# A fused transformer block: the first stage in another order, and Q scaled in whole half-groups

## The chip, the cores and the metric

The kernel runs on one core of one Trainium2 chip. The core has a matrix engine (TensorE, PE in the profile), a vector engine (VectorE, DVE), an activation engine (ScalarE, ACT), GpSimd (POOL), a queue engine (SyncE, SP) and 16 DMA engines. Each engine runs its own list of instructions in order and waits at semaphores for the others. The metric is device time in microseconds for one launch: the median of 3 runs of the kernel before is 843.28 us (843.05 to 843.71).

## The reference

Inputs are in bfloat16: tokens x of 2048 by 1024, a conditioning vector c, and the weights. The block is

```python
mod = (_silu(c) @ w_mod).reshape(c.shape[0], 6, 1, -1)
sa, ca, ga, sb, cb, gb = ...                     # six vectors of 1024
h = _layernorm(x) * (1 + ca) + sa
x = x + ga * _A_ref(h, A_wqkv, A_wo)             # linear attention, 32 heads of 32
h = _layernorm(x) * (1 + cb) + sb
x = x + gb * _B_ref(h, B_w_gate, B_w_up, B_w_down)   # gelu(h@w_gate) * (h@w_up) @ w_down, F = 3584
```

The attention has no softmax. With phi(t) = (t + 1 if t > 0 else exp(t)) + 1e-6, each head forms kv = phi(K)^T V (32 by 32) and z = the sum of phi(K) over tokens, and its output is phi(Q) kv / (phi(Q) z + 1e-6), which goes through wo.

## The kernel before

The 2048 tokens lie in SBUF as 16 chunks of 128 (`XALL`); four chunks make a token group of 512 (`sg` 0 to 3). The kernel keeps a list of instructions for each engine. A small scheduler (`Sched`) records which bytes each instruction reads and writes and derives the semaphore waits; the order on each engine is the order in which the Python code emits the instructions. Nothing reorders them later. DMAs go through SP; each takes one of 8 lanes in turn and waits for the DMA before it on its lane. DMAs issued from ACT would take one of 2 lanes.

**First stage (lines 429 to 746).** SP issues c, the first four token chunks one by one, `w_mod` in quarters (`wmq_dma(q)`: 256 columns of the shift and 256 of the scale, two DMAs of 512 KB), the K weights `wk` in row pairs, the V weights `wv` in column halves. For each of chunks 0 to 3, DVE computes layer norm statistics (`ln1_bn`, twice for a chunk, and `ln1_fin`), POOL raises the variance to -0.5, DVE normalises (`xhat_dve`), PE transposes (`t1`, eight 128 by 128 transposes into one PSUM bank), ACT copies the result into `H1` (L521), and DVE applies the modulation to it row tile by row tile (`mod1`, L538). The modulation vectors come quarter by quarter from PE (`mod_cols(q)`, 32 one-column matmuls, bank 4) and DVE (`mod_copy`). With quarter q, row tiles 2q and 2q+1 of the K projection can run: `k_part(q, chunks)`. Seven of the eight 128 by 512 K tiles of chunks 0 to 3 accumulate in banks 0 to 3 and 5 to 7 over all quarters; the eighth (chunk 3, second half) uses bank 4. `warm(n)` issues n matmuls of zeros on PE. When a K tile is whole, `k_evac` computes phi: ACT exp (L601), DVE min (L602), DVE add (L604). Then the V tiles follow in banks 0 to 3 in turn (`kv_mm`, `v_evac`), and `kvacc` accumulates kv and z in banks 5 to 7.

**Middle.** Chunks 4 to 15 repeat K, V and kvacc, with two 128 by 512 Q blocks for each chunk (`q_block`, evacuated by phi into `PQ[sg]`).

**Scaling of Q (lines 848 to 917).** Twelve Q blocks remain. `den` computes phi(Q) z for two token groups on PE, DVE inverts it (L854), SP stores the reciprocals to DRAM and loads them again broadcast over partitions into `RB[sg % 2]` (`rb_load`, L867, eight DMAs of 256 KB for a group, four for each half of its tokens). `pq_scale(sg, h, gs)` multiplies half h of group sg by them: one DVE instruction (L880) for two of the eight head groups, so four for a whole half. `kvbd` masks kv to its block diagonal (three DVE instructions), `kvt` transposes it (eight PE transposes in bank 4 and an ACT copy), and `w2_pair(g)` folds it into wo (two PE matmuls, an ACT copy into `W2`).

**Output projection (lines 932 to 988).** `wo_chunk(c)` runs 16 matmuls for each chunk, in banks 6 and 7 for chunk 0 and then in banks 2 and 3 or 0 and 1 in turn; DVE adds the result to `XALL` (L941), which frees the banks. For chunks 0 to 3, ACT and POOL compute the second layer norm and SP issues a DMA transpose into `H2` (`ln2_a`, T2). After chunk 9 DVE applies the second modulation (`mod2`). Chunks 12 to 15 are projected later, between gate/up pairs.

**Feed-forward.** For each group 28 tiles of gate and up (`ffn_fc`, L1003 and L1006) and the down projection (`ffn_down`, L1031), with the weights streamed by SP.

Of the kernel before, what the change touches and what calls it, by code (L numbers as in the profile page):

```python
# [12 lines left out]
D = 1024  # L13
# [201 lines left out]
def bass_adaLN_cond__linear_attn_block__geglu_ffn__prompt_kernel(  # L215
# [15 lines left out]
    with ExitStack() as es:  # L231
# [79 lines left out]
        def r_sm(name):  # L311
            return [(SMO[name], SMO[name] + SMSZ[name], name)]
# [7 lines left out]
        def r_xs(c0, c1):  # L320
            return [(OFF_XALL + c0 * D * 2, OFF_XALL + c1 * D * 2, "xall")]
# [104 lines left out]
            gop(lambda e, k=k: e.memset(bm32f[32 * k:32 * (k + 1), 8 * k:8 * k + 33 * 7 + 1:33], 1.0), wr=r_sm("bm32"))  # L426


        sch.dma(Q, lambda e: e.dma_start(C8[:], c_v), wr=r_sm("c8"), note="c8")

        def x_dma(c0, c1):
            return sch.dma(Q, lambda e: e.dma_start(XALL[:, c0:c1, :], x_v[:, c0:c1, :]), wr=r_xs(c0, c1), note=f"x{c0}")
# [14 lines left out]
        sch.op(V, lambda e: e.memset(ADD4[:, 0:2], 0.0), wr=r_sm("add4"), note="add4")  # L447
        sch.op(V, lambda e: e.memset(ADD4[:, 2:4], 1.0), wr=r_sm("add4"), note="add4")
        x_dma(0, 1)
        x_dma(1, 2)  # L450
        wmq_dma(0, (1,))
        x_dma(2, 3)
        wmq_dma(0, (0,))
        x_dma(3, 4)
        w_dma(WK, OFF_WK, "wk", 1, 0, D, 0, 2)
        for q in range(1, 4):
            wmq_dma(q)
            w_dma(WK, OFF_WK, "wk", 1, 0, D, 2 * q, 2 * q + 2)
        w_dma(WV, OFF_WV, "wv", 2, 0, 512)
        w_dma(WV, OFF_WV, "wv", 2, 512, 1024)  # L460
        x_dma(4, 8)
        w_dma(WQ, OFF_WQ, "wq", 0, 0, 512)
# [203 lines left out]
        def warm(n, bank=None):  # L666
            for _ in range(n):
                sch.op(T, lambda e: e.matmul(PS(0 if bank is None else bank), WARM[:, 0:P], WARM[:, :], start=bank is not None,  # L668
                                             stop=bank is not None, skip_group_check=True),
                       rd=R_WARM, pwr=pr(bank) if bank is not None else (), note="warm")  # L670
# [11 lines left out]

        kb0 = {(0, 0): 0, (0, 1): 1, (1, 0): 2, (1, 1): 3, (2, 0): 5, (2, 1): 6, (3, 0): 7}

        def k_part(q, cs):
            for dc in (2 * q, 2 * q + 1):
                for (c_, jg), b in kb0.items():
                    if c_ in cs:
                        kv_mm(c_, "k", jg, b, [dc])
# [42 lines left out]
        k_part(2, [0, 1, 2])  # L732
        mod_cols(3, 4)
        mod1(0, 4, 6, 8)
        k_part(2, [3])
        warm(2)
        k_part(3, [0, 1, 2, 3])
        for (c_, jg), b in kb0.items():
            k_evac(c_, jg, b)
        kv_mm(3, "k", 1, 4, list(range(NDC)))  # L740
        k_evac(3, 1, 4)
        for c_ in range(4):
            for jg in range(2):
                b = nb()
                kv_mm(c_, "v", jg, b, list(range(NDC)))
                v_evac(c_, jg, b)
            if c_ == 0:
                ln1(4)
                for k, t in enumerate((4, 5, 10, 11)):
                    wm_dma(t, k)  # L750
            if c_ >= 1:
                kvacc(c_ - 1)
            if c_ == 1:
                ln1(5)
            if c_ == 2:
                ln1(6)
                x_dma(12, 16)
                t1d(6)
                t1(4, 4)
                mod1(4, 1)  # L760
# [72 lines left out]
        def w2_pair(g, b0=2):  # L833
            for half in range(2):
                b = b0 + half
                sch.op(T, lambda e, b=b, half=half: e.matmul(PS(b), KVT[:, g, :], WO[:, g, half * 512:(half + 1) * 512], start=True, stop=True),  # L836
                       rd=R_KVT + [(OFF_WS + g * 2048 + half * 1024, OFF_WS + g * 2048 + (half + 1) * 1024, "wo")], pwr=pr(b), note=f"w2 {g}.{half}")
            sch.op(A, lambda e: e.activation(W2[:, g, :], ps_all[:, b0 * 512:(b0 + 2) * 512], ACTF.Copy),
                   prd=pr(b0) + pr(b0 + 1), wr=r_w(OFF_WK, "w2", g), note=f"w2cp{g}")
# [30 lines left out]
                        wr=r_rb(i, h) if k == 0 else (), deps=made[0].deps if k else [o_rd[sg // 2]], note=f"rb{sg}.{h}.{k}"))  # L870
                rb_ops[sg, h] = made

        GH = [((0, 2), (2, 4)), ((4, 6), (6, 8))]

        def pq_scale(sg, h, gs):
            i, t0 = sg % 2, h * HW
            for g0, g1 in gs:
                ap = PQ[sg][:, g0:g1, t0:t0 + HW]
                rng = r_pq(sg, g0, g1, t0, t0 + HW)
                sch.op(V, lambda e, ap=ap, i=i, h=h, g0=g0, g1=g1: e.tensor_tensor(ap, ap, RB[i][:, h, g0:g1, :], ALU.mult),  # L880
                       rd=rng + r_rb(i, h, g0, g1), wr=rng, deps=rb_ops[sg, h], note=f"pqs{sg}.{h}.{g0}")
# [19 lines left out]
        kvbd()  # L901
        q_next()
        q_next()
        for u in range(NG):
            q_next()
            if u == 0:
                kvt()
            else:
                w2_pair(u - 1)
            if u in (2, 3):  # L910
                pq_scale(0, 0, GH[u - 2])
            if u in (5, 6):
                pq_scale(0, 1, GH[u - 5])
        w2_pair(NG - 1, 4)
        assert not q_todo

        wd_q = [0]
# [56 lines left out]
        for c_ in range(12):  # L974
            wo_chunk(c_, 6 if c_ == 0 else 2 * (c_ % 2))
            if c_ == 0:
                den(1, 4)
                rb_load(2)
            if 1 <= c_ <= 8:
                pq_scale(1 + (c_ - 1) // 4, (c_ - 1) // 2 % 2, GH[(c_ - 1) % 2])  # L980
            if c_ == 4:
                rb_load(3)
            if c_ in (10, 11):
                pq_scale(3, 0, GH[c_ - 10])
            if c_ < 4:
                ln2_a(c_, False)
            if c_ == 9:
                mod2(0, 2)
                mod2(2, 2)
# [160 lines left out]
```

## Time and profile before

| what | value |
|---|---|
| median of 3 runs | 843.28 us (843.05 to 843.71) |
| the profiled execution | 843.05 us, its span 841.3 us |
| PE busy | 830.7 us, 99% of the span |
| DVE, ACT, POOL busy | 492.0, 294.9, 24.4 us |
| first V matmul, first output projection, first gate matmul on PE | 31.40, 201.47, 244.00 us |
| fillers (`warm`) on PE | 32, the first twelve from 2.31 us |
| one 128x512 phi: exp, min, add | 0.60, 0.43, 0.69 us |
| one scaling (L880), one addition (L941) | 0.68, 1.22 us |

The span goes from the first to the last instruction of the profiled execution; its own time is 1.75 us longer. All times in the lines below count from the start of the span. A line of the order of time gives start, duration, engine, source line, operation, what is written and read, and how many instructions were merged; in square brackets stand the idle time before it and what ended it. The matmuls overlap on PE, so the pace (start to start) of a 512-column matmul is 0.216 us, although one takes 0.379 us from start to end. "SPq" lines are DMA issues; their duration is that of the issue. A line of the transfers gives the size and the time from issue to landing.

### The profile page before, as it was taken

What the parts mean: (1) busy time and instruction counts of PE and PEld (TensorE: products, weight loads), DVE (VectorE), ACT (ScalarE), POOL (GpSimd) and SP (SyncE); (2) the same over time, 40 slices, a digit from 0 to 9 for tenths busy, and PEclk for the clock granted to TensorE, in tenths of its full rate; (3) what the DMA queues carried; (4) which work ended last, traced back from release to release, by engine and by line L of the source; (5) the groups of instructions that cost most, each with busy time, mean ns of one, the idle gap of its engine ahead of it and who ended that gap; (6) DMA issues with size and microseconds to landing.
All of it is one profiled execution on the core that took longest, in us unless ns stands there. A gap on an engine that the chain in (4) does not pass through costs nothing.

```text
span 841.3 us, 11255 instructions
## 1 busy us (share of the span) xinstructions
PE 830.7 (99%) x4149; PEld 387.9 (46%) x4229; DVE 492.0 (58%) x883; ACT 294.9 (35%) x483; POOL 24.4 (3%) x64
## 2 busy tenths in 40 slices
PE   8999999999999999999999999999999999999998
PEld 4454444444444444444444444444444444444445
DVE  5666767867785555654455665346666535655522
ACT  2343333335513344420355442044444104445300
POOL 2000000000200000010000001000000000000000
PEclk9999999999999999999999999999999999999999
DMA  9991824029778587340555533055553305555000
GB/s 286 354 285 26 263 47 105 14 54 233 165 165 252 155 253 206 105 97 23 149 153 154 153 102 69 26 157 150 150 151 101 75 19 158 152 157 141 7 19 26
DMA packets 181750, 112.70 MB, mean 134 GB/s; under 512 B 33080, under 2 KB 172728, under 8 KB 180672
## 3 DMA queue, kind: packets, MB, share of 16 engines
q1 hardware_dynamic: 181696, 111.98, 49.0%
q8 instruction: 34, 0.56, 0.3%
q14 instruction: 20, 0.16, 0.1%
HBM read 100.67 MB, written 4.47 MB: 125 GB/s over the span
## 4 chain that ended last, share of the span: by engine, by line
PE 96%; DVE 2%; issue 1%; ACT 1%; DMA 0%; ACTq 0%
PE ps_all L1006 23%; PE ps_all L1031 23%; PE ps_all L1003 22%; PE ps_all L612 12%; PE ps_all L934 7%; PE ps_all L653 6%; PE ps_all L668 1%; PE ps_all L634 1%; DVE h1T L538 1%; PE ps_all L584 0%; PE ps_all L836 0%; PE ps_all L565 0%; PE ps_all L519 0%; DVE ww L1019 0%; DVE ww L1016 0%
## 5 line engine op out<-in xcount | busy, mean ns | idle before, releaser
L1006 PE MATMUL ps_all<-h2T,wu 128*128 128x512 bf16 x896 | 339.6, 379 | 2.0
L1003 PE MATMUL ps_all<-h2T,wg 128*128 128x512 bf16 x859 | 325.6, 379 | 0.0
L1031 PE MATMUL ps_all<-wd,yT 128*128 128x512 bf16 (+1 forms) x907 | 193.2, 372 | 0.9
L1014 ACT ACTIVATE q<-ps_all 128x512 f32<-128x512 f32 x112 | 66.9, 597 | 229.4 <-PE ps_all L1003 224.5
L1031 PEld LDWEIGHTS ps_all<-wd,yT 128*128 128x128 bf16 x924 | 90.4, 98 | 103.2
L1003 PEld LDWEIGHTS ps_all<-h2T,wg 128*128 128x128 bf16 x896 | 87.7, 98 | 105.8 <-issue 0.2
L1006 PEld LDWEIGHTS ps_all<-h2T,wu 128*128 128x128 bf16 x896 | 87.7, 98 | 105.6
L1016 DVE SCALAR_TENSOR_TENSOR ww<-q,ps_all 128x512 f32<-128x512 f32 x112 | 77.0, 688 | 88.2 <-ACT guh L1015 88.2
L1019 DVE SCALAR_TENSOR_TENSOR ww<-th,guh 128x512 f32<-128x512 f32 x112 | 77.6, 693 | 77.9 <-ACT th L1018 77.9
L1018 ACT ACTIVATE th<-ww 128x512 f32<-128x512 f32 x112 | 70.5, 630 | 85.8 <-DVE ww L1016 85.8
L1021 DVE TENSOR_TENSOR yT<-ww,ps_all 128x512 bf16<-128x512 f32 x112 | 76.9, 687 | 3.8
L1036 DVE TENSOR_TENSOR ps_all<-ps_all,gbb 128x512 f32<-128x512 f32 (+1 forms) x33 | 22.5, 683 | 94.8 <-PE ps_all L1031 94.8
L1015 ACT ACTIVATE guh<-ps_all 128x512 f32<-128x512 f32 x112 | 66.3, 592 | 0.0
L601 ACT ACTIVATE eb<-ps_all 128x512 f32<-128x512 f32 x64 | 37.5, 601 | 77.9 <-PE ps_all L612 37.8
L653 PE MATMUL ps_all<-h1T,wq 128*128 128x512 bf16 x245 | 56.8, 379 | 1.4 <-DVE pq L604 0.7
L612 PE MATMUL ps_all<-wv,h1T 128*128 128x512 bf16 x254 | 57.8, 379 | 0.2
L612 PE MATMUL ps_all<-wk,h1T 128*128 128x512 bf16 x251 | 57.6, 379 | 0.2
L934 PE MATMUL ps_all<-w,pq 128*128 128x512 bf16 x251 | 56.0, 379 | 0.3
L602 DVE TENSOR_SCALAR eb<-eb 128x512 f32<-128x512 f32 x64 | 27.1, 424 | 34.0 <-ACT eb L601 33.6
L934 PEld LDWEIGHTS ps_all<-w,pq 128*128 128x128 bf16 x256 | 25.0, 98 | 30.2 <-issue 0.2
L612 PEld LDWEIGHTS ps_all<-wv,h1T 128*128 128x128 bf16 x256 | 24.9, 98 | 30.0 <-DVE eb L602 0.6
L612 PEld LDWEIGHTS ps_all<-wk,h1T 128*128 128x128 bf16 x256 | 24.6, 98 | 29.8 <-DVE h1T L538 1.5
(81 smaller groups left out, 398.8 us busy)
## 6 DMA issues: line engine op xcount, KB each, us to landing
wg<-in_B_w_gate_dram SPq DMA_DIRECT2D x56, 512.0 KB, 4.1
wu<-in_B_w_up_dram SPq DMA_DIRECT2D x56, 512.0 KB, 5.3
wmst<-in_w_mod_dram SPq DMA_DIRECT2D x8, 1024.0 KB, 11.6
rb<-scr_rd SPq DMA_DIRECT2D x32, 256.0 KB, 6.9
wd<-in_B_w_down_dram SPq DMA_DIRECT2D x7, 1024.0 KB, 7.6
wmq<-in_w_mod_dram SPq DMA_DIRECT2D x8, 512.0 KB, 7.0
out_dram<-xall SPq DMA_DIRECT2D x31, 128.0 KB, 1.7
xall<-in_A_x_dram SPq DMA_DIRECT2D x3, 1024.0 KB, 11.9
```

Of the source, the lines that this page charges most:

```text
L612: o = sch.op(T, lambda e, dc=dc: e.matmul(PS(bank), H1[sg][:, dc, ci * P:(ci + 1) * P], W_[:, dc, jg * 512:(jg + 1) * 512], start=(dc == 0 ...
L653: o = sch.op(T, lambda e, dc=dc: e.matmul(PS(b), WQ[:, dc, qc * P:(qc + 1) * P], H1[sg][:, dc, :], start=(dc == 0), stop=(dc == NDC - 1)), ...
L934: last[half] = sch.op(T, lambda e, g=g, half=half: e.matmul(PS(b0 + half), PQ[sg][:, g, ci * P:(ci + 1) * P], W2[:, g, half * 512:(half + ...
L1003: og = sch.op(T, lambda e, dc=dc: e.matmul(PS(bg), WG[slot][:, dc, e_ * P:(e_ + 1) * P], H2[sg][:, dc, :], start=(dc == 0), stop=(dc == ND ...
L1006: ou = sch.op(T, lambda e, dc=dc: e.matmul(PS(bu), WU[slot][:, dc, e_ * P:(e_ + 1) * P], H2[sg][:, dc, :], start=(dc == 0), stop=(dc == ND ...
L1014: sch.op(A, lambda e: e.activation(Q1[j][:, :], PS(bg), ACTF.Square, scale=math.sqrt(GELU_A)), prd=pr(bg), wr=rq, note=f"q1 {fc}")
L1015: ogh = sch.op(A, lambda e: e.activation(GUH[j][:, :], PS(bg), ACTF.Copy, scale=0.5), prd=pr(bg), wr=rg, note=f"gh {fc}")
L1016: sch.op(V, lambda e: e.scalar_tensor_tensor(WW[j][:, :], Q1[j][:, :], 1.0, PS(bg), op0=ALU.add, op1=ALU.mult), rd=rq, prd=pr(bg), wr=rw, ...
L1018: sch.op(A, lambda e: e.activation(TH[j][:, :], WW[j][:, :], ACTF.Tanh, scale=GELU_C), rd=rw, wr=rt, note=f"th {fc}")
L1019: sch.op(V, lambda e: e.scalar_tensor_tensor(WW[j][:, :], TH[j][:, :], 1.0, GUH[j][:, :], op0=ALU.add, op1=ALU.mult), rd=rt + rg, wr=rw, n ...
L1021: sch.op(V, lambda e: e.tensor_tensor(YT[:, fc, :], WW[j][:, :], PS(bu), ALU.mult), rd=rw, prd=pr(bu), wr=r_yt(fc), note=f"yT {fc}")
L1031: o = sch.op(T, lambda e, b=b, fc=fc, c0=c0, c1=c1, n=n: e.matmul(PS(b, 0, n), YT[:, fc, ci * P:(ci + 1) * P], WDT[fc // 4][:, fc % 4, c0:c1],
```

## The change

Two stretches are reordered; no arithmetic changes.

First stage: c and the second token chunk are issued from ACT. On SP the whole first modulation quarter stands ahead of the third chunk, the first `wk` pair ahead of the fourth; the last `wk` pair goes row tile by row tile, the first `wv` half in two row halves. On PE the first modulation quarter is computed before the transposes of chunk 1, K of chunk 0 starts before chunk 2 is transposed, fillers are fewer (26 for 32), the eighth K tile runs with the others (six row tiles ahead of the last two `wk` row tiles), and the V tiles of chunks 0 and 1 are interleaved. On DVE the modulation of chunk 0, then of chunk 1, stands ahead of the second statistics of chunk 2.

Second stretch: `pq_scale` does a whole half at a time (four instructions). `kvt` runs before the loop, `w2_pair(u)` follows its own Q block. The halves are scaled after u = 3 and 5, then at projection chunks 0 and 1 (group 1), 4 and 5 (group 2), 6 and 7 (group 3); before, in pairs of instructions at u = 2, 3, 5, 6, chunks 1 to 8, 10 and 11, and just ahead of the feed-forward. `rb_load(3)` moves from chunk 4 to chunk 1.

```diff
-        sch.dma(Q, lambda e: e.dma_start(C8[:], c_v), wr=r_sm("c8"), note="c8")
+        sch.dma(A, lambda e: e.dma_start(C8[:], c_v), wr=r_sm("c8"), note="c8")
...
         x_dma(0, 1)
-        x_dma(1, 2)
-        wmq_dma(0, (1,))
+        x_dma(1, 2, A)
+        wmq_dma(0, (1, 0))
         x_dma(2, 3)
-        wmq_dma(0, (0,))
+        w_dma(WK, OFF_WK, "wk", 1, 0, D, 0, 2)
         x_dma(3, 4)
-        w_dma(WK, OFF_WK, "wk", 1, 0, D, 0, 2)
         for q in range(1, 4):
             wmq_dma(q)
-            w_dma(WK, OFF_WK, "wk", 1, 0, D, 2 * q, 2 * q + 2)
-        w_dma(WV, OFF_WV, "wv", 2, 0, 512)
+            for d0, d1 in ((2 * q, 2 * q + 2),) if q < 3 else ((6, 7), (7, 8)):
+                w_dma(WK, OFF_WK, "wk", 1, 0, D, d0, d1)
+        w_dma(WV, OFF_WV, "wv", 2, 0, 512, 0, 4)
+        w_dma(WV, OFF_WV, "wv", 2, 0, 512, 4, 8)
         w_dma(WV, OFF_WV, "wv", 2, 512, 1024)
...
-        def k_part(q, cs):
-            for dc in (2 * q, 2 * q + 1):
+        def k_part(q, cs, dcs=(0, 1)):
+            for dc in [2 * q + k for k in dcs]:
...
         t1(0, 5)
-        warm(7, 7)
         ln1_bn(1, 1)
         ln1_fin(1)
+        warm(4, 7)
+        mod_cols(0, 4, False)
+        xhat_dve(1, *xh_buf(1))
+        mod_copy(0, 4)
+        mod1(0, 1, 0, 2)
+        t1(1, 6)
         ln1_bn(2, 0)
-        xhat_dve(1, *xh_buf(1))
-        t1(1, 6)
-        warm(1, 7)
-        mod_cols(0, 4, False)
-        warm(6, 7)
+        warm(3, 7)
+        k_part(0, [0])
+        mod1(1, 1, 0, 2)
         ln1_bn(2, 1)
         ln1_fin(2)
+        k_part(0, [1])
         ln1_bn(3, 0)
         xhat_dve(2, *xh_buf(2))
-        mod_copy(0, 4)
-        mod1(0, 2, 0, 2)
         t1(2, 7)
+        warm(5)
         ln1_bn(3, 1)
         ln1_fin(3)
         mod1(2, 1, 0, 2)
-        k_part(0, [0, 1])
+        k_part(0, [2])
         xhat_dve(3, *xh_buf(3))
-        k_part(0, [2])
+        mod_cols(1, 4)
         t1(3, 7)
-        mod_cols(1, 4)
         mod1(0, 3, 2, 4)
+        warm(2)
+        k_part(1, [0, 1, 2])
         mod1(3, 1, 0, 4)
-        warm(3)
-        k_part(1, [0, 1, 2])
...
-        warm(1)
         k_part(2, [0, 1, 2])
         mod_cols(3, 4)
         mod1(0, 4, 6, 8)
         k_part(2, [3])
-        warm(2)
-        k_part(3, [0, 1, 2, 3])
+        kv_mm(3, "k", 1, 4, list(range(6)))
+        for d in (0, 1):
+            k_part(3, [0, 1, 2, 3], (d,))
+            kv_mm(3, "k", 1, 4, [6 + d])
         for (c_, jg), b in kb0.items():
             k_evac(c_, jg, b)
-        kv_mm(3, "k", 1, 4, list(range(NDC)))
         k_evac(3, 1, 4)
         for c_ in range(4):
-            for jg in range(2):
+            for vc, jg in (((0, 0), (1, 0)), ((0, 1), (1, 1)), ((2, 0), (2, 1)), ((3, 0), (3, 1)))[c_]:
...
-        GH = [((0, 2), (2, 4)), ((4, 6), (6, 8))]
-
-        def pq_scale(sg, h, gs):
+        def pq_scale(sg, h, gs=((0, 2), (2, 4), (4, 6), (6, 8))):
...
+        kvt()
         for u in range(NG):
             q_next()
-            if u == 0:
-                kvt()
-            else:
-                w2_pair(u - 1)
-            if u in (2, 3):
-                pq_scale(0, 0, GH[u - 2])
-            if u in (5, 6):
-                pq_scale(0, 1, GH[u - 5])
-        w2_pair(NG - 1, 4)
+            w2_pair(u)
+            if u in (3, 5):
+                pq_scale(0, (u - 3) // 2)
...
-            if 1 <= c_ <= 8:
-                pq_scale(1 + (c_ - 1) // 4, (c_ - 1) // 2 % 2, GH[(c_ - 1) % 2])
-            if c_ == 4:
+            if c_ in (0, 1):
+                pq_scale(1, c_)
+            if c_ == 1:
                 rb_load(3)
-            if c_ in (10, 11):
-                pq_scale(3, 0, GH[c_ - 10])
+            if c_ in (4, 5, 6, 7):
+                pq_scale(2 + (c_ - 4) // 2, c_ % 2)
...
-        pq_scale(3, 1, GH[0] + GH[1])
```

More of the change, by code (lines that the diff above doesn't have):

```diff
@@ L426, in bass_adaLN_cond__linear_attn_block__geglu_ffn__prompt_kernel, with x_dma @@
             gop(lambda e, k=k: e.memset(bm32f[32 * k:32 * (k + 1), 8 * k:8 * k + 33 * 7 + 1:33], 1.0), wr=r_sm("bm32"))
-        sch.dma(Q, lambda e: e.dma_start(C8[:], c_v), wr=r_sm("c8"), note="c8")
-        def x_dma(c0, c1):
-            return sch.dma(Q, lambda e: e.dma_start(XALL[:, c0:c1, :], x_v[:, c0:c1, :]), wr=r_xs(c0, c1), note=f"x{c0}")
+        sch.dma(A, lambda e: e.dma_start(C8[:], c_v), wr=r_sm("c8"), note="c8")
+        def x_dma(c0, c1, stream=Q):
+            return sch.dma(stream, lambda e: e.dma_start(XALL[:, c0:c1, :], x_v[:, c0:c1, :]), wr=r_xs(c0, c1), note=f"x{c0}")
         def wm_dma(t, sl):
@@ L735, in bass_adaLN_cond__linear_attn_block__geglu_ffn__prompt_kernel @@
         k_part(2, [3])
-        warm(2)
-        k_part(3, [0, 1, 2, 3])
+        kv_mm(3, "k", 1, 4, list(range(6)))
+        for d in (0, 1):
+            k_part(3, [0, 1, 2, 3], (d,))
+            kv_mm(3, "k", 1, 4, [6 + d])
         for (c_, jg), b in kb0.items():
             k_evac(c_, jg, b)
-        kv_mm(3, "k", 1, 4, list(range(NDC)))
         k_evac(3, 1, 4)
         for c_ in range(4):
-            for jg in range(2):
+            for vc, jg in (((0, 0), (1, 0)), ((0, 1), (1, 1)), ((2, 0), (2, 1)), ((3, 0), (3, 1)))[c_]:
                 b = nb()
-                kv_mm(c_, "v", jg, b, list(range(NDC)))
-                v_evac(c_, jg, b)
+                kv_mm(vc, "v", jg, b, list(range(NDC)))
+                v_evac(vc, jg, b)
             if c_ == 0:
@@ L831, in kvt, with w2_pair @@
             sch.op(A, lambda e: e.activation(KVT[:].rearrange("p a b -> p (a b)"), PS16(4), ACTF.Copy), prd=pr(4), wr=R_KVT, note="kvt")
-        def w2_pair(g, b0=2):
+        def w2_pair(g):
+            b0 = 2
             for half in range(2):
```

## The prediction

> **What bounds the kernel now.** I read the page first, then the chain that ended last, then each engine's instructions in order of time in the two stretches that the change touches: 0 to 46 us (first stage) and 176 to 245 us (scaling of Q, output projection). Last I read the transfers, issue by issue.
>
> The page's busy times and its row of granted clock:
>
> ```profile
> span 841.3 us, 11255 instructions
> PE 830.7 (99%) x4149; PEld 387.9 (46%) x4229; DVE 492.0 (58%) x883; ACT 294.9 (35%) x483; POOL 24.4 (3%) x64
> PEclk9999999999999999999999999999999999999999
> ```
>
> PE is the bound from end to end: whatever makes PE wait lengthens the span, and whatever shortens another engine gains nothing unless PE waited for it. Thirty-two of PE's instructions are fillers (`warm`, zeros times zeros); dropping one gains 0.216 us only if no wait takes its place.
>
> PE in 8 to 18 us (start, duration):
>
> ```profile
> 9.70 0.61 PE L519 MATMUL ps_all<-ident,xh 128*128 128x128 bf16 x8
> 10.37 0.94 PE L565 MATMUL ps_all<-siluT,wmq 128*128 128x1 bf16 x32
> 11.38 1.24 PE L668 MATMUL ps_all<-warm 128*128 128x512 bf16 x5
> 12.46 0.61 PE L519 MATMUL ps_all<-ident,xh 128*128 128x128 bf16 x8
> 12.91 2.75 PE L612 MATMUL ps_all<-wk,h1T 128*128 128x512 bf16 x12
> ```
>
> DVE in the same time:
>
> ```profile
> 9.50 0.69 DVE L674 BATCH_NORM_STATS2 st<-xall 128x6 f32<-128x512 bf16 x1
> 11.48 0.53 DVE L494 TENSOR_SCALAR xh<-xall,mv,rs 128x1024 bf16<-128x1024 bf16 x1
> 11.93 0.15 DVE L576 TENSOR_TENSOR modt<-ps_all,add 128x4 f32<-128x4 f32 x1
> ```
>
> The reader is to see that the statistics of chunk 2 (9.50) run before the modulation (11.93), so its transpose can start at 12.46, the moment PE has run out of fillers.
>
> The second stretch, DVE and then SP:
>
> ```profile
> 191.77 1.28 DVE L880 TENSOR_TENSOR pq<-pq,rb 128x512 bf16<-128x512 bf16 x2
> 230.39 1.23 DVE L941 TENSOR_TENSOR xall<-ps_all,xall 128x1024 bf16<-128x1024 f32 x1 [1.03 <-PE ps_all L934]
> 216.99 0.42 SPq L867 DMA_DIRECT2D rb<-scr_rd  x1
> 217.52 15.70 SPq L528 DMA_TRANSPOSE h2T<-xh  x4
> 233.31 3.78 SPq L867 DMA_DIRECT2D rb<-scr_rd  x8
> ```
>
> Two scalings (1.28) fit between two evacuations, four do not always. The reciprocals of token group 3 are issued at 233.31, far from any user. The landings, each from one issue (first and last reciprocal piece of group 2, first transpose):
>
> ```profile
> rb<-scr_rd SPq DMA_DIRECT2D x1, 256.0 KB, 3.0
> rb<-scr_rd SPq DMA_DIRECT2D x1, 256.0 KB, 8.6
> h2T<-xh SPq DMA_TRANSPOSE x1, 9.0
> ```
>
> Issued at 213.82, 216.99 and 217.52 they land at 216.8, 225.6 and 226.5: eight pieces, 1.2 us apart, then the transpose. From 218 to 224 us the 16 DMA engines are 98% busy. These pieces move at 1.2 us each, one behind another.
>
> **First stage, part by part.** All PE prices are paces from the rows: a 512-column matmul 0.216, eight transposes 0.45, a modulation quarter 0.78.
>
> 1. c and the second tokens from ACT; bytes reordered. SP's rows show 0.41 for each of the two issues, so later transfers start up to 0.9 us sooner. ACT's table load (1.28, at 0.72) moves behind the two issues, so siluT, ready at 3.1, can be 0.8 late. That is covered: DVE would first wait for x0 (3.92), and the first transposes wait for the twelfth filler at 7.41, 0.45 after xhat. Price 0. The extra issues (wk and wv in more pieces) cost SP about 0.4 each, hidden because SP runs 6 to 8 us ahead of the landings. The third and fourth tokens now land at about 10.2 and 12.4 at the latest (8.4 and 10.9 before); DVE asks for them at 10.7 and 13.0.
> [...]
>
> 2. First modulation quarter before the transposes of chunk 1. Its two pieces landed at 7.7 and 10.2; by bytes in the new order the second comes at 9.3, or 8.8 with the earlier start. PE: first transposes 7.41 to 8.19, four fillers to 9.05, quarter to 9.83, transposes of chunk 1 to 10.28. ACT copies them 10.49 to 11.51 (1.02).
>
> 3. The new wait. DVE's order is now copy (10.04), modulation of chunk 0, first statistics of chunk 2 (to 11.35), modulation of chunk 1, which waits for ACT until 11.55. Behind it stand the second statistics of chunk 2 (0.67), aggregate (0.24), POOL's power (0.13+0.57) and xhat (0.55): done at 14.34, so transposes at 14.44, where they were at 12.46. PE has only eight K matmuls before them (11.16 to 12.89): **1.56 idle**. Then transposes and five fillers to 15.97; ACT's copy ends at 16.11, the modulation of chunk 2 lets K go at 16.54: **0.57 idle**.
>
> 4. From 16.54 PE is full: 56 K matmuls 12.08, three quarters 2.34, transposes 0.45, two fillers 0.43, small waits 0.1: K ends at 31.9, against 31.4. All landings but the last (wk row 7, 26.5 or sooner) are well ahead.
>
> 5. Eighth K tile merged. Before, its 8 matmuls came after the other seven tiles were complete and covered the first evacuation (exp 28.58, bank 0 free at 30.36, needed at 31.40). Now tile 0 finishes at 30.54 and exp, min, add (1.78 together) free bank 0 at 32.35: V starts 32.41, **0.53 idle**. The new V order only saves the wait for the second wv half (0.1 us at 33.29). Second V tile at 34.14 against 33.38: **+0.78**. Six fillers (1.29) went and 2.1 of idle came. Bounds: if nothing but landings limited (step 3 absent), the second V tile starts at 32.8, -0.6; if the first quarter lands 0.5 later than I put it, +1.2. I take +0.78, the value that the DVE chain gives.
>
> PE's new gap could close the clock. Before shows matmuls 0.4255 apart until 7.41 and 0.216 after, and no later gap over 0.66. If a gap halved the clock for as long as at the start (5.1 us), it would cost 2.5. [...] I take nothing, as both neighbouring gaps are short.
>
> **Second stretch.** Counts do not change: 32 scalings, 16 w2 matmuls, 32 reciprocal pieces.
>
> 6. kvt before the loop: its transposes wait for kvbd (three DVE parts to 183.74) about 0.6 instead of the 0.66 that the next Q block waited at 185.26. Price 0. w2 of the last group goes to banks 2 and 3, copied in time (203 against 205).
>
> 7. Four scalings in a row (4 x 0.6 = 2.4) behind the evacuation of Q block u=3, 194.0 to 196.4: the evacuation of u=4 ends at 197.5 and the Q block u=6, due at 196.9, starts at 197.6: **0.74**. The output projection starts at 201.9, not 201.47: +0.45.
>
> 8. Projection. Groups 1 and 2 are scaled in time: PE takes 3.45 per chunk, DVE 1.14 for the addition and 2.4 more in two chunks of four, and PSUM leaves one chunk of slack. Group 3 is now scaled at chunks 6 and 7. Its eight pieces are issued after the first T2 transpose, moved past the other three T2 transposes and one gate/up pair on SP. The queue decides their landing: after the transpose at 226.5, one per 1.2: first half at 231.3, second at 236.1. DVE asks for the first at 229.2. Addition 7 waits behind that scaling to 233.7; addition 8 behind the second, 236.1+2.4, and ends at 239.8. Projection 10 needs the banks of addition 8: it starts at 239.85 where it started at 237.1: **+2.75** for the whole stretch, the 0.45 of step 7 swallowed. Bounds: transpose not in the way, 0.9 less; pieces held until that transpose begins (225.4, then 3.5 for the first) or the store of the reciprocals late with its DVE work, 1.2 and 0.5 more. T2 transposes 1 to 3 then land at 237 to 240, and mod2 of chunks 2 and 3 is due at 242.7: hidden by 3 us, beyond which each us counts.
>
> 9. Behind 245 us nothing is left to absorb it: gate and up run without a gap. DVE's six scalings at 243.7 to 249.7 are gone, but PE did not wait for them: 0.
>
> Sum: 0.78 + 2.75 = +3.5. The profiled execution took 843.05 (span 841.3, 1.75 around it), 0.23 under the median 843.28; 846.6 by the one, **846.8** by the other.
>
> **Rivals.**
> - Not slower: the reciprocals of group 3 come before DVE asks, because their issue moves 14 us ahead. Then step 8 leaves 0.5 and the total is +1.3, 844.6: within 0.2% (1.7 us, about what this kernel's measurement can tell). It decides from 2 us earlier than my 236.1. For it: SP is free at 218.8. Against it: the 98% busy queue.
> - First stage ruled by landings, -0.6 as bounded: +2.15, 845.4. For it: before, PE met each quarter's landing (25.12, 26.45). Against it: the DVE chain of step 3.
> - Pieces held behind the transpose (step 8's upper bound, +1.2): 848.0. The second transpose's issue took 6.5 us, so SP can be held there.
> - The clock falls in the gap: +2.5, 849.3.
>
> **How the numbers follow.** Main case 0.63, rivals 0.10, 0.08, 0.13, 0.06. Range 844.4 to 849.2: all but about 1 in 10. Slower by over 0.2%: 0.88 (all cases but the first rival, less the low edge); within: 0.09; faster: 0.03, both parts missing at once.
>
> **What would show it.** Right: the transposes of chunk 2 (L519) near 14.4 with idle before them on PE; first V matmul waiting for DVE; a Q block near 197 waiting for DVE; DVE idle near 229 to 231 with additions 7 and 8 late, and PE waiting twice near 234 and 239. Wrong: scalings of group 3 without a wait before them, or K ending before 31.4.

## The result, and the profile after

The changed kernel takes 847.91 us (median of 4 runs, 847.74 to 847.99); the kernel before, on the same chip, 843.27 (843.05 to 843.71). The ratio is 1.0054, with a 95% interval of 1.0037 to 1.0072: slower by 4.6 us, where +3.5 was forecast.

PE is still the bound and does the same work in the same time (830.9 us busy, 830.7 before); its waits lengthened the span. From the page of the changed kernel:

```profile
span 846.2 us, 11248 instructions
PE 830.9 (98%) x4144; PEld 386.5 (46%) x4223; DVE 492.3 (58%) x885; ACT 294.8 (35%) x483; POOL 24.4 (3%) x64
```

PE of the changed kernel in the first stage, in order of time (start, duration, engine, line, operation, operands, count; in brackets the idle time before and what ended it):

```profile
8.59 0.95 PE L566 MATMUL ps_all<-siluT,wmq 128*128 128x1 bf16 x32
9.41 0.61 PE L520 MATMUL ps_all<-ident,xh 128*128 128x128 bf16 x8
10.72 1.89 PE L613 MATMUL ps_all<-wk,h1T 128*128 128x512 bf16 x8
13.95 0.62 PE L520 MATMUL ps_all<-ident,xh 128*128 128x128 bf16 x8 [1.34 <-DVE xh L495]
16.03 1.04 PE L613 MATMUL ps_all<-wk,h1T 128*128 128x512 bf16 x4 [0.39 <-DVE h1T L539]
31.94 7.08 PE L613 MATMUL ps_all<-wv,h1T 128*128 128x512 bf16 x32 [0.37 <-DVE pk L605]
```

All three waits that the prediction named are there: for chunk 2's xhat (1.34; forecast 1.56), for its modulation (0.39; 0.57), for bank 0 (0.37; 0.53). The first V matmul comes at 31.94, 0.54 later than before.

PE of the changed kernel in the second stretch:

```profile
197.98 1.90 PE L654 MATMUL ps_all<-h1T,wq 128*128 128x512 bf16 x8 [0.65 <-DVE pq L605]
202.31 3.62 PE L931 MATMUL ps_all<-w,pq 128*128 128x512 bf16 x15
206.84 27.80 PE L931 MATMUL ps_all<-w,pq 128*128 128x512 bf16 x125
236.86 12.22 PE L931 MATMUL ps_all<-w,pq 128*128 128x512 bf16 x47 [2.22 <-DVE xall L938]
248.92 0.38 PE L1000 MATMUL ps_all<-h2T,wg 128*128 128x512 bf16 x1
```

Before, PE ran through the same stretch without a wait, up to the gates at 244.00:

```profile
206.00 38.16 PE L934 MATMUL ps_all<-w,pq 128*128 128x512 bf16 x172
```

DVE of the changed kernel in the projection: each scaling of group 3 waits for its reciprocals, and the addition that frees PE's banks stands behind it.

```profile
229.61 1.22 DVE L938 TENSOR_TENSOR xall<-ps_all,xall 128x1024 bf16<-128x1024 f32 x1
233.17 2.50 DVE L882 TENSOR_TENSOR pq<-pq,rb 128x512 bf16<-128x512 bf16 x4 [2.35 <-DMA rb<-scr_rd]
235.59 1.22 DVE L938 TENSOR_TENSOR xall<-ps_all,xall 128x1024 bf16<-128x1024 f32 x1
238.08 2.50 DVE L882 TENSOR_TENSOR pq<-pq,rb 128x512 bf16<-128x512 bf16 x4 [1.28 <-DMA rb<-scr_rd]
240.50 1.22 DVE L938 TENSOR_TENSOR xall<-ps_all,xall 128x1024 bf16<-128x1024 f32 x1
```

SP of the changed kernel: group 3's eight pieces go out from 219.34 (233.31 before), behind one transpose.

```profile
217.97 1.27 SPq L529 DMA_TRANSPOSE h2T<-xh  x1
219.34 9.02 SPq L871 DMA_DIRECT2D rb<-scr_rd  x8
229.37 9.43 SPq L529 DMA_TRANSPOSE h2T<-xh  x3
```

The gates start at 248.92 against 244.00, +4.92: +0.30 up to the first matmul of `kvacc` (38.86 against 38.56), +0.54 from there to the output projection, and +4.08 from the projection to the gates (46.61 against 42.53). Behind the gates nothing comes back.

PE's wait of 2.22 also closed the clock, to 0.50 in the third stretch below. The changed kernel in four stretches of 3.41 us, with PE's busy time first and the granted clock behind POOL:

```profile
231.23:234.64 3.41, 3.41 (x16) 1.37 (x14) 1.47 (x3) 1.24 (x1) 0.91 (x3) 1.00 1.12 231
234.64:238.05 3.41, 1.19 (x7) 0.60 (x7) 2.17 (x3) 0.00 (x0) 0.00 (x0) 1.00 1.00 191
238.05:241.46 3.41, 3.41 (x10) 1.22 (x9) 3.38 (x5) 0.00 (x0) 0.00 (x0) 0.50 0.96 200
241.46:244.87 3.41, 3.41 (x18) 1.52 (x16) 2.91 (x8) 0.00 (x0) 0.00 (x0) 1.00 0.97 265
```

So two things are in this trace that the sum did not have: a fallen clock, and landings later than the sum put them (233.05 and 237.96 against 231.3 and 236.1; 0.84 of each difference is the later start of the projection).

### The profile page after: what moved, and what is told of

It reads as the page before. It is cut to its first block, busy times and chain, and to the rows that moved or that the text cites. A ratio compares the mean times of both kernels' runs of the same rounds, so it can differ in the third digit from the quotient of the medians.

```text
span 846.2 us, 11248 instructions
## 1 busy us (share of the span) xinstructions
PE 830.9 (98%) x4144; PEld 386.5 (46%) x4223; DVE 492.3 (58%) x885; ACT 294.8 (35%) x483; POOL 24.4 (3%) x64
## 4 chain that ended last, share of the span: by engine, by line
PE 92%; DVE 3%; DMA 3%; ACT 1%; issue 1%; SPq 0%; POOL 0%; DVEq 0%; ACTq 0%
PE ps_all L1003 23%; PE ps_all L1028 23%; PE ps_all L1000 21%; PE ps_all L613 12%; PE ps_all L654 6%; PE ps_all L931 3%; DMA rb<-scr_rd 2%; PE ps_all L635 1%; PE ps_all L669 1%; DVE h1T L539 1%; DVE pq L882 1%; DMA scr_rd<-rdc 1%; PE ps_all L585 0%; PE ps_all L566 0%; PE ps_all L520 0%
## 5 line engine op out<-in xcount | busy, mean ns | idle before, releaser
L931 PE MATMUL ps_all<-w,pq 128*128 128x512 bf16 x251 | 57.8, 387 | 2.5 <-DVE xall L938 2.2
```

Of the source, the lines that this page charges most:

```text
L931: last[half] = sch.op(T, lambda e, g=g, half=half: e.matmul(PS(b0 + half), PQ[sg][:, g, ci * P:(ci + 1) * P], W2[:, g, half * 512:(half + ...
```

## The experiments

Medians of 2 to 11 runs; the kernel before ran beside each (843.17 to 843.34).

| kernel | median us | ratio to before, 95% | projection to gates |
|---|---|---|---|
| before | 843.27 | | 42.53 |
| changed | 847.91 | 1.0037 to 1.0072 | 46.61 |
| first_only | 843.50 | 0.9994 to 1.0013 | |
| second_only | 846.43 | 1.0025 to 1.0053 | 45.57 |
| scale3_late | 844.07 | 1.0001 to 1.0020 | 42.54 |
| extra_pieces | 851.62 | 1.0078 to 1.0119 | 50.54 |
| keep_warm | 847.77 | 1.0037 to 1.0071 | 46.31 |
| after_sp | 848.81 | 1.0045 to 1.0079 | 46.36 |
| fetch_shift | 846.81 | 1.0029 to 1.0056 | 44.91 |
| stats_first | 843.81 | 0.9994 to 1.0013 | |
| kvt_early | 843.00 | 0.9987 to 1.0006 | |
| tile8_tail | 843.43 | 0.9991 to 1.0009 | |
| best1 | 842.37 | 0.9979 to 0.9997 | |
| early_fill | 842.55 | 0.9982 to 1.0000 | |

### The two halves, each alone (first_only, second_only)

The lines of one half are put back; the cut is at `w2_pair`. First the changed first stage with the old second stretch:

```diff
-        kvt()
         for u in range(NG):
             q_next()
-            w2_pair(u)
-            if u in (3, 5):
-                pq_scale(0, (u - 3) // 2)
+            if u == 0:
+                kvt()
+            else:
+                w2_pair(u - 1)
...
-            if c_ == 1:
+            if c_ == 4:
                 rb_load(3)
```

> The first stage as changed, the second stretch as before. My account (fillers gone, but the transposes of chunk 2 late and bank 0 late): the profile of the changed kernel puts the first kvacc 0.30 later than before, so 843.6 us, +0.3 on 843.28, and the granted clock stays full. Rival (all of the cost lies in the second stretch, and the earlier landings of the first stage carry through): 842.7 or less. Rival (the first stage's waits also cost the stages behind it): 844.5 or more.

Measured: 843.50, +0.29 against 843.21, within what can be told from no change. Then the old first stage with the changed second stretch:

```diff
-        x_dma(1, 2, A)
-        wmq_dma(0, (1, 0))
+        x_dma(1, 2)
+        wmq_dma(0, (1,))
         x_dma(2, 3)
-        w_dma(WK, OFF_WK, "wk", 1, 0, D, 0, 2)
+        wmq_dma(0, (0,))
         x_dma(3, 4)
...
```

> The first stage as before, the second stretch as changed. My account: the output projection starts 0.5 later, then PE waits for the scaling of group 3, gates start 4.6 later than before: 847.6 us. Rival (the parts interact, the second stretch suffers from the shift of the first): 846.5 or less.

Measured: 846.43, +3.22, and 1.2 under what was expected: it is the rival's number, so the two parts interact. PE waits at the same two places as in the changed kernel:

```profile
236.32 3.63 PE L928 MATMUL ps_all<-w,pq 128*128 128x512 bf16 x16 [1.43 <-DVE xall L935]
241.21 7.08 PE L928 MATMUL ps_all<-w,pq 128*128 128x512 bf16 x31 [1.26 <-DVE xall L935]
```

The halves add up to 3.5 and the whole costs 4.64: 1.1 us appear only when both are there. In the traces they lie between the projection and the gates (46.61 against 45.57).

### Where the projection's wait comes from (scale3_late, extra_pieces)

Only group 3's scaling is moved to where its reciprocals have long landed:

```diff
-            if c_ in (4, 5, 6, 7):
-                pq_scale(2 + (c_ - 4) // 2, c_ % 2)
+            if c_ in (4, 5):
+                pq_scale(2, c_ % 2)
+            if c_ in (10, 11):
+                pq_scale(3, c_ % 2)
```

> The changed kernel with only the scaling of group 3 moved from projection chunks 6 and 7 to 10 and 11; its loads stay where the change has them, and the four-instruction groups too. My account (DVE stands at the scaling until the reciprocals land, and the additions behind it hold PE's banks): no wait of DVE for these loads, gates start 0.85 later than before, 844.1 us, and the granted clock stays full. Rival (the loads in SP's order are what costs, since three T2 transposes stand behind them): 846 or more. Rival (four scalings in a row are what costs): 846 or more.

Measured: 844.07, and the projection to the gates takes 42.54, as before the change. The projection runs through without a wait:

```profile
202.32 3.62 PE L931 MATMUL ps_all<-w,pq 128*128 128x512 bf16 x15
206.86 38.16 PE L931 MATMUL ps_all<-w,pq 128*128 128x512 bf16 x172
244.86 0.38 PE L1002 MATMUL ps_all<-h2T,wg 128*128 128x512 bf16 x1
```

The whole loss behind the projection's start, clock and all, hangs on these two instruction groups. What stays, 0.86, is the first stage and the 0.54 ahead of the projection. Then two more pieces of 256 KB, whose data nothing uses, ahead of group 3's eight:

```diff
             if c_ == 1:
+                for k in range(2):
+                    sch.dma(Q, lambda e, k=k: e.dma_start(
+                        WQ[32 * k:32 * (k + 1), 0:4, :].rearrange("p a b -> p (a b)").bitcast(f32),
+                        scr_rd[2, 0, k:k + 1, 0:2048].to_broadcast([32, 2048])),
...
                 rb_load(3)
```

> The changed kernel with two more pieces of 256 KB loaded ahead of those of group 3, into bytes that nothing reads. My account (each piece moves the landing of group 3 by 1.2 us, and the landing sets the end): 850.3 us, +2.4 on the changed kernel. Rival (DVE's own work sets the end, the landing is covered): 847.9, no change.

Measured: 851.62, 1.3 more than expected. The last piece landed at 38.51 after the projection's start in place of 35.65, +2.86 for two pieces. PE of this kernel, and its clock in two stretches of 3.41 us (0.50 in both):

```profile
239.51 13.13 PE L931 MATMUL ps_all<-w,pq 128*128 128x512 bf16 x47 [4.96 <-DVE xall L938]
```

```profile
237.98:241.39 3.41, 1.88 (x5) 0.73 (x6) 2.29 (x4) 0.00 (x0) 0.00 (x0) 0.50 1.13 220
241.39:244.81 3.42, 3.42 (x10) 1.21 (x8) 2.81 (x4) 0.00 (x0) 0.00 (x0) 0.50 0.95 231
```

From the landing of the last piece to the gates: 10.73 in second_only, 10.96 in the changed kernel, 12.03 here. The first is scaling, addition and two projections; what is above it is the half clock's part, 0.23 in the changed kernel and 1.3 here. These 1.1 more, and pieces that cost 2.86 in place of 2.4, make up the miss.

### Is it the clock? (keep_warm)

Ten unused matmuls (L974) fill PE's wait:

```diff
         for c_ in range(12):
+            if c_ == 9:
+                for _ in range(10):
+                    sch.op(T, lambda e: e.matmul(PS(5), W2[:, 0, 0:P], W2[:, 0, 0:512], start=True, stop=True, ...), ...)
```

> Kernel: the changed kernel with ten added matmuls of 512 columns (2.16 us, into the free bank 5) in PE's wait of 2.22 us between projections 8 and 9; they compute nothing that is used. Theory: the clock stays open through 238 to 242, but the time that the half clock cost lay almost wholly under the second wait for the reciprocals, so the median moves by -0.3 to 0: 847.6 to 847.9, and the gates still start about 10.7 after the landing of the last piece. Rival: the clock that fell at 238.05 is what the prediction lacked: 1.5 us or more faster, 846.4 or less.

Measured: 847.77. The clock stayed at 1.0 and the gates start 10.72 after the landing, but the time is the changed kernel's: the second wait ends with the landing at either clock.

```profile
234.52 2.32 PE L974 MATMUL ps_all<-w 128*128 128x512 bf16 x10
236.87 3.63 PE L931 MATMUL ps_all<-w,pq 128*128 128x512 bf16 x16
241.75 7.08 PE L931 MATMUL ps_all<-w,pq 128*128 128x512 bf16 x32 [1.25 <-DVE xall L938]
```

### The 1.1 us that only the whole change loses (after_sp, fetch_shift)

From the landing of group 2's first piece to that of the first transpose takes 9.7 us before, 9.8 in second_only, and 10.8 to 10.9 in the changed kernel, scale3_late, extra_pieces and keep_warm. Group 3's pieces stand behind that transpose. The first theory was ACT's queue:

```diff
-        sch.dma(A, lambda e: e.dma_start(C8[:], c_v), ...)
+        sch.dma(Q, lambda e: e.dma_start(C8[:], c_v), ...)
...
-        x_dma(1, 2, A)
+        x_dma(1, 2)
```

> Kernel: the changed kernel with c and the second token chunk issued from SP again. Theory: the issuer has nothing to do with the second stretch; 847.5 to 848.3, and the time from the landing of the first reciprocal piece of group 2 to the landing of the first transpose into h2T stays at 10.8 us. Rival: once ACT has issued a DMA, its queue keeps a share of the DMA engines' turns and the later transfers go slower: that time falls to 9.8, the pieces of group 3 land 1.0 sooner, and the total is 846.6 to 847.0.

Measured: 848.81 (848.20 to 848.93), and still 10.8. The issuer is not the cause. The total is 0.9 above the changed kernel's, above the expected range too; the profiled execution (848.20) starts its gates at 248.91, so where the rest went is open.

The transfers themselves show another candidate. Packets of the changed kernel from 224.6 to 224.8 us (by queue: packets, MB, share):

```profile
DMA packets 143, 0.05 MB, mean 259 GB/s; under 512 B 142, under 2 KB 142, under 8 KB 142
q1 hardware_dynamic: 142, 0.04, 121.2%
q8 instruction: 1, 0.02, 48.3%
```

The 142 small packets are the first transpose; the one of 16 KB is on the queue that the profile calls instruction (q8). It takes 1.55 us from 224.66, and the next stretches of the same kernel show what the rest did meanwhile (last two columns: DMA share, GB/s):

```profile
224.50:225.75 1.25, 1.25 (x7) 0.59 (x6) 1.13 (x1) 0.00 (x0) 0.00 (x0) 1.00 2.60 159
225.75:227.00 1.25, 1.25 (x8) 0.56 (x6) 0.00 (x0) 0.00 (x0) 0.00 (x0) 1.00 0.06 6
```

The transfers stand nearly still for 1.2 us, where second_only, whose packet went out at 221.15, moves 212 GB/s in the same stretch:

```profile
225.75:227.00 1.25, 1.25 (x8) 0.54 (x7) 0.48 (x2) 0.00 (x0) 0.00 (x0) 1.00 0.73 212
```

A page of either kernel counts 34 such packets; in the changed one there are 4144 + 4223 recorded PE instructions, 246 to a packet. From these counts the author took it for PE's code, fetched as PE goes along: an estimate, by which its place can be shifted by lengthening PE's list. Sixteen one-column matmuls (32 instructions with their weight loads), hidden in PE's idle 1.3 us in the first stage, do that:

```diff
         xhat_dve(2, *xh_buf(2))
+        for _ in range(16):
+            sch.op(T, lambda e: e.matmul(PS(7, 0, 1), WARM[:, 0:P], WARM[:, 0:1], start=True, stop=True, ...), ...)
         t1(2, 7)
```

> Kernel: the changed kernel with sixteen added one-column matmuls of zeros on PE, in its wait before the transposes of chunk 2 (16 x 0.0245 = 0.4 us of the 1.3 idle there); they compute nothing that is used. They move every later instruction of PE's code 32 places on. Theory: the 1 us that the transfers lose in the whole change, and in neither half of it alone as much, is PE's code being fetched: one packet of 16 KB (queue q8, 1.55 us) at 224.66, inside the first transpose into h2T, where before had it at 219.06 among the reciprocal pieces and the second stretch alone at 221.15. PE runs about 250 recorded instructions between two such packets, 32 in 3.45 us in the projection: with 32 more ahead, the packet comes 3 us or more sooner, the transpose lands 9.7 to 9.9 after the first piece of group 2 (10.8 in the changed kernel), the pieces of group 3 land 1.0 sooner, and the total is 846.6 to 847.1. Rival (the packet is a passenger): the transpose lands 10.8 after, the total is 847.7 to 848.1.

Measured: 846.81 (846.68 to 847.38; the changed kernel 847.74 to 847.99), 1.1 faster with more work. The packet went out 19.16 us after the projection's start in place of 22.35 (222.50), among the reciprocal pieces, and the transpose landed 9.9 after the first of these. The transfer view of the changed kernel, and then of fetch_shift, gives the time from the issue of that transpose to its landing:

```profile
h2T<-xh SPq DMA_TRANSPOSE x1, 10.1
```

```profile
h2T<-xh SPq DMA_TRANSPOSE x1, 9.1
```

PE's first wait shrinks from 2.22 to 0.76, the second stays:

```profile
236.44 3.63 PE L934 MATMUL ps_all<-w,pq 128*128 128x512 bf16 x16 [0.76 <-DVE xall L941]
241.33 7.08 PE L934 MATMUL ps_all<-w,pq 128*128 128x512 bf16 x32 [1.26 <-DVE xall L941]
```

The packet is shown to cost about 1 us in that place (10.1 against 9.1), and it came 3.19 us sooner with 32 more instructions in PE's list ahead of it; that it holds PE's code is still an estimate. (From the projection to the gates fetch_shift takes 44.91 in place of 46.61: 1.0 is the shorter transpose, 0.23 the clock that stayed open, and 0.5 an earlier issue of the whole queue, 15.17 against 15.66 after the projection's start for the transpose, which is not the packet's doing.)

The other traces say why both halves are needed. The packet goes out at 16.59 to 18.59 after the projection's start in the three executions with the first stage of before, and the transpose lands 9.7 to 9.8 after the first piece. In nine with the changed first stage it goes out at 22.35 to 23.04, and the transpose lands 10.4 to 10.9 after: in first_only, stats_first, tile8_tail and best1 too, where no reciprocals of group 3 stand behind it and the delay costs PE nothing. (In early_fill it goes out at 22.26, but the pieces were issued 0.6 later than in best1, so it fell among them, and the transpose took 9.8.) So the first half moves the packet, and the second makes PE wait for what stands behind the transpose. Why the six fillers that the changed first stage drops moved it by 3.8 us against second_only (18.59 after the projection's start there) is not shown: the packets come 162 to 320 recorded PE instructions apart in the traces of the kernel before and the changed one.

### The terms of the first stage and of the w2 stage (stats_first, tile8_tail, kvt_early)

Each is measured in the traces from the first transposes (the first tokens) to the first V matmul: 23.99 before, 24.82 in the changed kernel, 24.98 in first_only. These numbers hold something that is not the order's: the eight first transposes themselves, which take 0.45 once the clock has opened and up to 0.84 before. Here they are with the fillers behind them in first_only (0.79 from the one start to the other), then in stats_first (0.44):

```profile
8.11 0.95 PE L520 MATMUL ps_all<-ident,xh 128*128 128x128 bf16 x8
8.90 1.03 PE L669 MATMUL ps_all<-warm 128*128 128x512 bf16 x4
```

```profile
7.53 0.61 PE L520 MATMUL ps_all<-ident,xh 128*128 128x128 bf16 x8
7.97 1.03 PE L669 MATMUL ps_all<-warm 128*128 128x512 bf16 x4
```

Counted from their end, the way to the first V matmul is 23.21 before and 24.19 to 24.36 in the five executions with this first stage as it is (first_only, the changed kernel, scale3_late, keep_warm, extra_pieces). Now chunk 2's statistics are put ahead:

```diff
-        mod1(1, 1, 0, 2)
         ln1_bn(2, 1)
         ln1_fin(2)
+        mod1(1, 1, 0, 2)
         k_part(0, [1])
```

> Kernel: the changed first stage with the second stretch of before, but chunk 2's second statistics and aggregate stand ahead of the modulation of chunk 1 on DVE. Theory (step 3's chain is real: the statistics waited behind a modulation that waits for ACT): the transposes of chunk 2 come about 1.0 us sooner than in the run with the changed first stage alone, at 13.5 to 14.1 against 15.10 there, PE's idle time before them is under 0.7 in place of 1.43, and the median falls by 0.2 to 0.5, to about 843.1 (843.5 there), no longer by 1.0, since the modulation of chunk 1 and the K tiles behind it move back by the same statistics. Rival (the first stage is ruled by the landings, not by this chain): PE meets the landings instead and the median stays at 843.5.

Measured: in the trace 24.26, 0.72 less than first_only, but 0.35 of that is the clock in the first transposes; from their end it is 23.82, 0.37 less, with the wait for xhat down to 0.23 and a new one of 0.77 for the modulation of chunk 1:

```profile
12.53 1.04 PE L613 MATMUL ps_all<-wk,h1T 128*128 128x512 bf16 x4 [0.77 <-DVE h1T L539]
13.80 0.62 PE L520 MATMUL ps_all<-ident,xh 128*128 128x128 bf16 x8 [0.23 <-DVE xh L495]
```

The median, 843.81 (842.61 to 844.33), shows nothing of this: that expectation missed. The chain is real, its worth in time below what these runs scatter. Next, the last two matmuls of the eighth tile behind the other seven:

```diff
-        for d in (0, 1):
-            k_part(3, [0, 1, 2, 3], (d,))
-            kv_mm(3, "k", 1, 4, [6 + d])
+        k_part(3, [0, 1, 2, 3])
+        kv_mm(3, "k", 1, 4, [6, 7])
```

> Kernel: the changed first stage with the second stretch of before, but the eighth K tile's last two row tiles come after the other seven tiles are whole. Theory of step 5: the four matmuls cover part of the evacuation of tile 0, so PE's wait of 0.36 before the first V matmul goes; from the first transposes to the first V matmul 24.6 to 24.8 us (24.98 in the run with the changed first stage alone, 23.99 before), median 843.2 to 843.4. Rival: the wait moves to the second V tile or to K, 24.9 to 25.0 and 843.5.

Measured: 24.66 in the trace, which scale3_late and keep_warm reach without this edit (24.64 each). From the end of the first transposes it is 23.98, 0.21 less, just what the wait at the first V matmul loses: 0.15 in place of 0.36. The wait shrinks and does not go; median 843.43. Last, the kernel before with only the transposes of kv moved:

```diff
+        kvt()
         for u in range(NG):
             q_next()
-            if u == 0:
-                kvt()
-            else:
-                w2_pair(u - 1)
+            w2_pair(u)
```

> Kernel: before, with only the transposes of kv moved ahead of the loop and each pair of w2 matmuls behind its own Q block; the scaling stays in pairs. Step 6 prices this at 0: 843.1 to 843.4, the projection at 201.4 to 201.6. Rival: the 0.54 us that the second stretch lost before the projection comes from this move and not from the four scalings in a row: 843.7 to 843.8, the projection at 202.0.

Measured: 843.00. From `kvacc` to the projection 162.63 us, 162.91 before: the move gains 0.28, since this Q block of before waits no more:

```profile
185.92 1.90 PE L653 MATMUL ps_all<-h1T,wq 128*128 128x512 bf16 x8 [0.66 <-DVE pq L604]
```

The changed second stretch takes 163.45 on the same way (alone and with the changed first stage), so four scalings in a row cost 0.82.

### A version without the waits (best1, early_fill)

The changed first stage with both repairs, `kvt` ahead of the loop, scaling in pairs as before:

```diff
-            if u in (3, 5):
-                pq_scale(0, (u - 3) // 2)
+            if u in (2, 3):
+                pq_scale(0, 0, GH[u - 2])
+            if u in (5, 6):
+                pq_scale(0, 1, GH[u - 5])
```

> Kernel: the changed first stage with both repairs (chunk 2's second statistics ahead of the modulation of chunk 1, the eighth tile's last two row tiles behind the others), the scaling of before in pairs, and the transposes of kv ahead of the loop. Theory: from the first transposes to the first V matmul 24.0 to 24.2 (23.99 before, 24.26 with the statistics first), nothing lost in the second stretch, so 842.7 to 843.2: the same as before within 0.2%, and no reason in the trace for more. Rival: the earlier first quarter and the smaller bytes ahead bring a gain that the two waits hid, 842.3 or less.

Measured: 842.37 (842.12 to 843.65, 11 runs), ratio 0.9988 with an interval of 0.9979 to 0.9997: about 1 us faster than before, and between the two forecasts. The trace does not account for it: `kvt` gains 0.28, and the first stage, 23.60 from the end of the first transposes, is 0.59 shorter than in first_only (0.37 and 0.21, the two repairs) but still 0.39 longer than before's. From the start of the first transposes it is 24.44, above the 24.0 to 24.2 expected, since they ran at the half clock (0.84). Four waits remain, 0.77, 0.23, 0.39 and 0.15; the first and the last:

```profile
12.74 1.04 PE L613 MATMUL ps_all<-wk,h1T 128*128 128x512 bf16 x4 [0.77 <-DVE h1T L539]
31.79 7.08 PE L613 MATMUL ps_all<-wv,h1T 128*128 128x512 bf16 x32 [0.15 <-DVE pk L605]
```

Its profiled execution took 843.01 (before's 843.05), one of its slower runs, so the gain lies in runs without a trace. One reading: before's own first stage met late landings in two of three profiled executions (0.93 and 0.84 of PE's time for `wmq` in kvt_early and second_only, 24.82 and 24.96 in all), and the new order of bytes lost 0.2 at the most to them. From the end of the first transposes to the first `kvacc` these two take 31.17 and 31.42, before's undisturbed one 30.37, best1 and early_fill 30.52 each. That fits, but for the runs without a trace it is argued, not shown. Then two more fillers ahead of the transpose of c, since the clock's opening scatters (5.9 to 8.8 us in the profiles) and could be what spreads the runs:

```diff
+        for _ in range(2):
+            sch.op(T, lambda e: e.matmul(PS(7), WARM[:, 0:P], WARM[:, :], start=True, stop=True, ...), ...)
         sch.op(T, lambda e: e.transpose(PS16(4, 0, NDC), C8[:, :], IDENT[0:NDC, 0:NDC]), ...)
```

> Kernel: the combined kernel (both repairs, scaling in pairs, kv transposed ahead of the loop) with two more fillers on PE ahead of the transpose of c, at about 1.15 us, where PE waits for c until 2.14 to 2.9. [...] Rival: the first tokens and the modulation's landings set the start, and the median stays at 842.3 to 842.5.

Measured: 842.55 (842.14 to 843.48). PE worked from 1.17 (2.14 in best1), stood still for 0.68 until c landed, and the clock opened at 8.12. The author's estimate, an opening about 1 us sooner and a median of 842.1, missed. What spreads the runs of one kernel is not settled.

## Why the prediction was right, and where it was wrong

Direction and range held (844.4 to 849.2); the point, 846.8, was 1.1 short, and the sum of 3.5 hides errors of both signs.

- **Steps 2 to 5, first stage.** The mechanism came as forecast, down to the three waits, and the price too, against the trace it was worked out from: from the end of the first transposes to the first `kvacc` the order costs 0.74 (31.11 in first_only, 30.37 before). What failed is the comparison: before was priced at its one undisturbed trace, and its other two executions lose as much to landings. By medians the stage costs 0.29, not 0.78. That the changed kernel's own trace shows 0.30 too is chance: its first transposes started 0.29 sooner (7.12, 7.41 before) and were 0.33 shorter, since the clock had opened before them (at 5.94; at 8.10 before, near their end). Step 1 (price 0) is open: with c and the second tokens on SP the total was 0.9 higher, the first stage no longer (24.83).
- **Step 6 (price 0).** It gains 0.28. The new wait is shorter than the one it replaces by more than the 0.06 of the estimate.
- **Step 7 (+0.74, net +0.45 at the projection).** The four scalings cost 0.82, with the Q block waiting 0.65; together with step 6, +0.54.
- **Step 8, the landings.** The forecast took its landings from before's trace; counted from the projection's start there they are 29.8 and 34.6 us for the two halves. second_only has 29.95 and 34.84. The queue's pace, 1.2 us a piece behind the transpose, was right (233.05 to 237.96 for four pieces), and with it both waits. Two terms were wrong. First, "the 0.45 of step 7 swallowed": the reciprocals are made after projection 0, so their landing moves with the projection's start and nothing is swallowed. Second, a term that was missing: the 16 KB packet in the middle of the transpose, +1.0 (10.1 from issue to landing, 9.1 in fetch_shift), which PE pays only in the whole change. The changed kernel's gates, 1.39 later than forecast (248.92 against 244.00 + 0.78 + 2.75), are these: 0.54 not swallowed, 1.0 for the packet, 0.23 for the clock, less 0.48 in the first stage, which leaves 0.1. "Groups 1 and 2 are scaled in time" held for PE alone: DVE waited 1.56 for group 2's second half (0.77 in second_only), and PE did not feel it.
- **T2's other transposes and step 9 (hidden).** Held: the gates started with the last projection's end in each kernel.
- **Rivals.** "Not slower" needed landings 2 us sooner; they came later. "Pieces held behind the transpose" gives 848.0, the nearest number by far, and is still the wrong reason: SP issued the pieces from 219.34, and the delay was in the transpose's own transfer, gone in fetch_shift with SP's order unchanged. "The clock falls in the gap" did happen, in the projection rather than in the first stage, and cost 0.23 rather than 2.5, since it fell while DVE, not PE, was the one to wait for.

On that clock: the granted clock was 0.50 for 3.41 us, and in the 3.41 us ahead of that PE worked 1.19. The wait of 2.22 was enough there, while second_only's 1.43 and 1.26, the first stage's 1.34 and even after_sp's 2.34 did not close it. That 1.56 of idle costs nothing was the author's estimate, and it held for the 1.34 that came: the clock stayed at 1.0.

## What to carry to other kernels

A wait for a transfer behind a queue moves with whatever starts that queue's chain: before calling a delay swallowed, look for what makes the data that is waited for. Move a consumer no further forward than its data: the same scaling four chunks later cost nothing. When two changes together cost more than apart, look in the packets for what only shifted, and when a trace of before is used as the base, know how another execution of the same order looks.

## What the runs showed of the hardware

- A 16 KB packet of the instruction queue (q8) took 0.88 to 1.55 us in the traces of the kernel before and the changed one (34 in each). Where it fell among the reciprocal pieces, the transpose behind them landed 9.7 to 9.9 us after the first piece; where it fell at the end of the pieces or inside the transpose, 10.4 to 10.9. The last of group 3's pieces, queued behind the transpose, landed 35.65 us after the projection's start in the changed kernel and 34.84 in second_only.
- After a wait of 2.22 us on PE the granted clock was 0.50 for 3.41 us (changed kernel), after one of 4.96 for two such stretches (extra_pieces). A wait of 2.34 (after_sp, up to 237.23) left it at 1.0. So by these runs the length of the wait alone does not decide; what else does is not shown. The clock opened 5.9 to 8.8 us after the start in the 13 profiled executions that recorded it: at 5.94 in the changed kernel, at 8.10 in the kernel before.
